# A fused attention and two-layer kernel: the first layer's inner columns in groups of 2, 2, 3, 3, 3 and 3 chunks

## Chip, cores and metric

The kernel runs on one core of a Trainium2 chip. The metric is the device time of one execution in microseconds (us); the number given for a kernel is the median of its runs. The trace is that of one profiled execution.

## What is computed

Linear attention over 4 sequences of 576 tokens and 8 heads of 64 (no softmax), a root-mean-square norm for each head, then a dense layer with an ELU, then four experts of which every token uses all, weighted by given probabilities:

```
kv  = einsum('bhsd,bhse->bhde', k, v);  o = einsum('bhsd,bhde->bhse', q, kv)
x   = o / sqrt(mean(o*o) + 1e-6) * g_norm          # 2304 tokens x 512
h   = x @ w_in                                      # 512 -> 2048
y   = elu(h) @ w_out                                # 2048 -> 512
out = sum_e p[:, e] * (relu(y @ w1[e]) @ w2[e])     # 512 -> 1024 -> 512, 4 experts
```

The weights `w_in` and `w_out` of the first layer arrive as 64-bit floats. All products are made from float32 operands split into a high part and a rest, so that a product takes three matmuls.

## The kernel before

Tokens go in 6 blocks of 384 (`NB` = 6, `T` = 384). The first layer's 2048 inner columns are 16 chunks of 128. `first_groups` says which chunks are summed in PSUM before the sum is added to the accumulator in SBUF: before, [0, 1], [2, 3], [4 to 7], [8 to 11], [12 to 15]. Group 0 runs inside the attention stage, whose order is written out by hand (`plan`). The other groups run in one list of steps: for each group, for each block j, for each chunk c of the group one step, 84 in all. A step is `emit_mm1` (12 matmuls of 384 columns into a bank of "ab", lines 425 to 427; then the ELU: ScalarE at lines 434 and 435, VectorE at line 439 in `end_elu`; then the split of the result into two parts, ScalarE at line 186, GpSimd at line 196) and, two steps later (`LAG`), `emit_mm2` (12 matmuls into four banks, lines 463 to 465). At a group's first chunk of a block `emit_mm2` takes four of the six banks "efghcd" in turn; at its last chunk `into_acc` adds the four banks to the accumulator of the block, one VectorE instruction each (line 457; for group 0 a ScalarE copy, line 455). I call this the turnover of a block.

The weights of a chunk are two pieces (`w_in` and `w_out`, 128 x 512). A piece is loaded into one of two `raw` buffers (line 140, queue of SyncE), turned from 64-bit to 32-bit floats by five VectorE instructions (lines 154, 157, 171, 179, 182) and two of ScalarE (165, 166), and split into a slot of the pool `w_p` (ScalarE line 186, GpSimd line 196). `w_p` has 17 slots (`NSLOT`). They also hold the second layer's weights: `stage_w1` makes sums of blocks of `w1` in one slot (`tf`, lines 219 to 222), `split_w1` fills four, `split_w2` one for each piece of `w2`, and the two sums `s` of `make_forms` take one each. A slot of the first layer comes free when the last block has used its piece.

`todo` holds what is emitted among the steps, by half step h: the pieces of the next group during a group, and during the last group the first preparation of the second layer. That is `stage_w1`/`split_w1` for the first two half groups of expert columns, `split_w2` for two pieces, and `one_form`, five times. `make_forms(0)` makes seven matrices (A11, S2, S1, A12, S3, A22, S4) from the finished accumulators of blocks 0 and 1, splits each on ScalarE (line 186) and GpSimd (line 196) into half of an `x_p` buffer, which it shares with the blocks' inputs `xq`, and stores each to DRAM. The second layer begins with `emit_q(0, 0, 0)`, whose first products (lines 505 to 507) read these forms. The place in `todo` sets a rank, not a time: the order on each engine is fixed when the program is built, and work whose inputs and buffers are there may stand ahead of its place.

Of the kernel before, what the change touches and what calls it, by code (L numbers as in the profile page):

```python
# [33 lines left out]
def attention_moe_kernel(  # L34
# [25 lines left out]
    NF = FG // P  # L60
# [6 lines left out]
    NB = NT // T  # L67
# [57 lines left out]

    w_in, w_out = w_in.bitcast(U32), w_out.bitcast(U32)
    NC1 = F1 // P
    first_groups = [[0, 1], [2, 3]] + [list(range(n, n + NF)) for n in range(NF, NC1, NF)]
    assert sum(map(len, first_groups)) == NC1
    NG = E * F2 // FG  # L130

# [592 lines left out]
    steps = []  # L724
    for g, cs in list(enumerate(first_groups))[1:]:
        begins = 2 * len(steps)
        steps += [(g, j, c) for j in range(NB) for c in cs]
        length = 2 * len(steps) - begins
        if g + 1 < len(first_groups):
            cs = first_groups[g + 1]  # L730
            pieces = [p for i in range(0, len(cs), 2) for p in ((0, cs[i]), (0, cs[i + 1]), (1, cs[i]), (1, cs[i + 1]))]
            for n, (ab, c) in enumerate(pieces):
                todo.setdefault(begins + length * (n + 3) // (len(pieces) + 4), []).append((split_w, 0, ab, c))
    def one_form():
        next(forms_of_0, None)

    for h, ops in ((6, [(stage_w1, 0, 0), (split_w1, 0, 0)]), (22, [(one_form,)]), (24, [(one_form,)]),
                   (28, [(one_form,)]), (32, [(one_form,)]), (36, [(one_form,)]),
                   (40, [(stage_w1, 0, 1), (split_w1, 0, 1)]), (46, [(split_w2, 0, 0)]), (48, [(split_w2, 0, 1)])):
        todo.setdefault(begins + h, []).extend(ops)  # L740

    forms_of_0 = make_forms(0)
# [102 lines left out]
```

## Time and profile before

| | us |
|---|---|
| median of 3 runs | 1224.46 (1224.4 to 1226.63) |
| profiled execution, its own time | 1225.07 |
| its span, first to last instruction | 1223.3 |
| TensorE (PE) busy in the span | 1205.8 |
| VectorE (DVE) busy | 627.8 |
| ScalarE (ACT) busy | 444.0 |
| GpSimd (POOL) busy | 350.4 |

The profiled execution took 1.8 us more than its span and 0.6 us more than the median. PEld in the rows is TensorE's weight load, SP the queue of SyncE. Matmuls are pipelined, so the busy time of one is about twice the distance from one to the next; lost time is better read from the number of matmuls in a stretch.

### The profile page before, as it was taken

What the parts mean: (1) busy time and instruction counts of PE and PEld (TensorE: products, weight loads), DVE (VectorE), ACT (ScalarE), POOL (GpSimd) and SP (SyncE); (2) the same over time, 40 slices, a digit from 0 to 9 for tenths busy, and PEclk for the clock granted to TensorE, in tenths of its full rate; (3) what the DMA queues carried; (4) which work ended last, traced back from release to release, by engine and by line L of the source; (5) the groups of instructions that cost most, each with busy time, mean ns of one, the idle gap of its engine ahead of it and who ended that gap; (6) DMA issues with size and microseconds to landing.
All of it is one profiled execution on the core that took longest, in us unless ns stands there. A gap on an engine that the chain in (4) does not pass through costs nothing.

```text
span 1223.3 us, 16937 instructions
## 1 busy us (share of the span) xinstructions
PE 1205.8 (99%) x6678; PEld 1122.4 (92%) x6678; DVE 627.8 (51%) x1071; ACT 444.0 (36%) x858; POOL 350.4 (29%) x311
## 2 busy tenths in 40 slices
PE   8899999999999999999999999999999999999998
PEld 8799999999999999999999999999999999999997
DVE  5777888474222526755445445445445445444443
ACT  3667666454344544332132132122123123122110
POOL 1223454253233744452032033023023023021000
PEclk9999999999999999999999999999999999999999
DMA  9611333120000312443442442441451451450562
GB/s 332 220 52 53 87 86 103 37 61 10 1 18 27 138 55 80 200 158 101 172 151 84 183 158 72 179 178 54 175 202 36 188 207 35 190 201 15 206 233 77
DMA packets 43887, 147.14 MB, mean 120 GB/s; under 512 B 7072, under 2 KB 7072, under 8 KB 43808
## 3 DMA queue, kind: packets, MB, share of 16 engines
q1 hardware_dynamic: 43808, 146.07, 33.6%
q8 instruction: 52, 0.85, 0.3%
q14 instruction: 27, 0.22, 0.1%
HBM read 124.82 MB, written 21.23 MB: 119 GB/s over the span
## 4 chain that ended last, share of the span: by engine, by line
PE 79%; DVE 2%; ACT 1%; issue 1%; DMA 0%; POOL 0%; DVEq 0%; POOLq 0%; ACTq 0%
PE ps_y L559 11%; PE ps_y L558 11%; PE ps_y L560 11%; PE ps_h L425 3%; PE ps_h L427 3%; PE ps_h L426 3%; PE ps_y L465 3%; PE ps_y L464 3%; PE ps_y L463 3%; PE ps_a L505 3%; PE ps_c L506 3%; PE ps_a L507 3%; PE ps_c L507 3%; PE ps_a L506 3%; PE ps_c L505 3%; PE ps_b L506 3%
## 5 line engine op out<-in xcount | busy, mean ns | idle before, releaser
L559 PE MATMUL ps_y<-w,h 128*128 128x512 f32 x576 | 226.2, 393 | 0.0
L558 PE MATMUL ps_y<-w,h 128*128 128x512 f32 x576 | 224.0, 391 | 0.4 <-DVE acc L571 0.4
L560 PE MATMUL ps_y<-w,h 128*128 128x512 f32 x576 | 220.1, 391 | 0.0
L532 POOL TENSOR_TENSOR c<-u,p 128x384 f32<-128x384 f32 x48 | 49.2, 1026 | 418.7 <-DVE h L544 418.7
L544 DVE SCALAR_TENSOR_TENSOR h<-c,h 128x384 fp32r<-128x384 f32 x144 | 97.6, 677 | 136.5 <-ACT h L543 136.5
L196 POOL TENSOR_TENSOR h<-e,h 128x384 fp32r<-128x384 f32 x96 | 104.0, 1085 | 197.8 <-ACT h L186 171.2
L543 ACT ACTIVATE h<-c 128x384 fp32r<-128x384 f32 x144 | 75.8, 527 | 199.3 <-POOL c L532 77.0
L425 PE MATMUL ps_h<-x,w 128*128 128x384 f32 x384 | 129.8, 338 | 1.4 <-DVE e L439 1.2
L465 PE MATMUL ps_y<-h,w 128*128 128x384 f32 x384 | 129.1, 336 | 0.7 <-POOL w L196 0.7
L463 PE MATMUL ps_y<-h,w 128*128 128x384 f32 x384 | 124.8, 338 | 5.0 <-DVE acc L457 2.5
L426 PE MATMUL ps_h<-x,w 128*128 128x384 f32 x384 | 128.5, 335 | 0.5 <-DVE x L401 0.5
L464 PE MATMUL ps_y<-h,w 128*128 128x384 f32 x384 | 128.8, 335 | 0.0
L427 PE MATMUL ps_h<-x,w 128*128 128x384 f32 x384 | 128.4, 334 | 0.0
L560 PEld LDWEIGHTS ps_y<-w,h 128*128 128x128 f32 x576 | 108.1, 188 | 21.7
L558 PEld LDWEIGHTS ps_y<-w,h 128*128 128x128 f32 x576 | 108.1, 188 | 19.6 <-DVE acc L571 0.8
L559 PEld LDWEIGHTS ps_y<-w,h 128*128 128x128 f32 x576 | 108.0, 188 | 19.4
L571 DVE SCALAR_TENSOR_TENSOR acc<-ps_y,p_sb,acc 128x512 f32<-128x512 f32 x126 | 87.6, 746 | 65.2 <-PE ps_y L560 65.1
L439 DVE SCALAR_TENSOR_TENSOR e<-e,ps_h 128x384 f32<-128x384 f32 x96 | 52.7, 550 | 114.9 <-ACT e L435 114.8
L521 ACT COPY p<-ps_c 128x384 f32<-128x384 f32 x48 | 23.1, 482 | 153.4 <-PE ps_c L507 153.4
L463 PEld LDWEIGHTS ps_y<-h,w 128*128 128x128 f32 x384 | 71.9, 188 | 7.2 <-DVE acc L457 3.8
L434 ACT ACTIVATE e<-ps_h 128x384 f32<-128x384 f32 x96 | 46.8, 487 | 84.9 <-PE ps_h L427 82.0
L425 PEld LDWEIGHTS ps_h<-x,w 128*128 128x128 f32 x384 | 72.1, 188 | 4.0 <-DVE e L439 3.6
(103 smaller groups left out, 2381.8 us busy)
## 6 DMA issues: line engine op xcount, KB each, us to landing
f<-kept SPq DMA_DIRECT2D x98, 768.0 KB, 7.5
raw<-in_moe_w_dram SPq DMA_DIRECT2D x64, 256.0 KB, 2.7
kept<-f SPq DMA_DIRECT2D x21, 768.0 KB, 3.3
raw<-in_moe_w_in_dram SPq DMA_DIRECT2D x16, 512.0 KB, 3.6
raw<-in_moe_w_out_dram SPq DMA_DIRECT2D x16, 512.0 KB, 3.7
qkv<-in_k_dram SPq DMA_DIRECT2D x18, 256.0 KB, 5.8
qkv<-in_v_dram SPq DMA_DIRECT2D x18, 256.0 KB, 5.6
qkv<-in_q_dram SPq DMA_DIRECT2D x18, 256.0 KB, 5.4
```

The lines of the kernel that those rows point to most:

```text
L196: eng.tensor_tensor(out=l, in0=x, in1=h, op=ALU.subtract)
L425: nc.tensor.matmul(ps, ah, bh, start=(kk == 0), stop=False)
L426: nc.tensor.matmul(ps, ah, bl, start=False, stop=False)
L427: nc.tensor.matmul(ps, al, bh, start=False, stop=(kk == KD - 1))
L463: nc.tensor.matmul(ps, bh[:, cols], hi, start=first, stop=False)
L464: nc.tensor.matmul(ps, bh[:, cols], lo, start=False, stop=False)
L465: nc.tensor.matmul(ps, bl[:, cols], hi, start=False, stop=last)
L506: nc.tensor.matmul(ps, wh, xl, start=False, stop=False, skip_group_check=True)
L544: nc.vector.scalar_tensor_tensor(out=lo, in0=ps, scalar=0.0, in1=hi.bitcast(F32), op0=ALU.max, op1=ALU.subtract,)
L558: nc.tensor.matmul(ps, hi[:, cols], bh, start=first, stop=False)
L559: nc.tensor.matmul(ps, hi[:, cols], bl, start=False, stop=False)
L560: nc.tensor.matmul(ps, lo[:, cols], bh, start=False, stop=last)
```

## The change

The inner groups become [4 to 6], [7 to 9], [10 to 12] and [13 to 15], so that there are six groups in place of five. The list that spreads the next group's pieces is written so that a group of odd length fits: the pieces of a pair of chunks, then those of the single one. The preparation of the second layer keeps its start, which is counted from the end of the list of steps as before (24 steps from the end), though the last group now begins 6 steps later; its five calls of `one_form` move from half steps 22, 24, 28, 32 and 36 to 28, 30, 32, 35 and 38, and the second `stage_w1` from 40 to 42.

```diff
-    first_groups = [[0, 1], [2, 3]] + [list(range(n, n + NF)) for n in range(NF, NC1, NF)]
+    first_groups = [[0, 1], [2, 3]] + [list(range(n, n + 3)) for n in range(4, NC1, 3)]
...
-            pieces = [p for i in range(0, len(cs), 2) for p in ((0, cs[i]), (0, cs[i + 1]), (1, cs[i]), (1, cs[i + 1]))]
+            pieces = [(ab, c) for i in range(0, len(cs), 2) for ab in (0, 1) for c in cs[i:i + 2]]
             for n, (ab, c) in enumerate(pieces):
                 todo.setdefault(begins + length * (n + 3) // (len(pieces) + 4), []).append((split_w, 0, ab, c))
+    begins = 2 * (len(steps) - NB * NF)
...
-    for h, ops in ((6, [(stage_w1, 0, 0), (split_w1, 0, 0)]), (22, [(one_form,)]), (24, [(one_form,)]),
-                   (28, [(one_form,)]), (32, [(one_form,)]), (36, [(one_form,)]),
-                   (40, [(stage_w1, 0, 1), (split_w1, 0, 1)]), (46, [(split_w2, 0, 0)]), (48, [(split_w2, 0, 1)])):
+    for h, ops in ((6, [(stage_w1, 0, 0), (split_w1, 0, 0)]), (28, [(one_form,)]), (30, [(one_form,)]),
+                   (32, [(one_form,)]), (35, [(one_form,)]), (38, [(one_form,)]),
+                   (42, [(stage_w1, 0, 1), (split_w1, 0, 1)]), (46, [(split_w2, 0, 0)]), (48, [(split_w2, 0, 1)])):
         todo.setdefault(begins + h, []).extend(ops)
```

## Rows read from the trace of the kernel before

**Rows 1.** The page's first part: busy time, share of the span, instructions.
```profile
PE 1205.8 (99%) x6678; PEld 1122.4 (92%) x6678; DVE 627.8 (51%) x1071; ACT 444.0 (36%) x858; POOL 350.4 (29%) x311
```

**Rows 2.** Busy time (and instructions) of PE, PEld, DVE, ACT, POOL by stretch.
```profile
122.00:174.00 52.00, 49.83 (x282) 48.38 (x281) 44.22 (x77) 31.01 (x59) 24.04 (x20) 1.00 0.32 91
174.00:228.00 54.00, 52.72 (x297) 50.87 (x296) 42.89 (x71) 34.84 (x66) 24.63 (x21) 1.00 0.30 89
228.00:250.00 22.00, 22.00 (x129) 22.00 (x128) 5.25 (x10) 8.32 (x17) 6.45 (x7) 1.00 0.00 1
250.00:280.00 30.00, 29.98 (x173) 29.66 (x172) 24.84 (x38) 19.01 (x37) 16.62 (x13) 1.00 0.25 70
280.00:400.00 120.00, 120.00 (x694) 120.00 (x693) 32.30 (x61) 46.93 (x93) 39.47 (x39) 1.00 0.04 12
400.00:434.00 34.00, 33.64 (x195) 33.26 (x194) 17.49 (x24) 18.04 (x34) 25.39 (x24) 1.00 0.37 145
434.00:472.00 38.00, 37.94 (x219) 37.62 (x219) 12.35 (x24) 15.85 (x32) 17.02 (x16) 1.00 0.15 45
```

**Rows 3.** Waits of PEld from 122 to 472: total us, times, longest.
```profile
PEld ps_y L463 <- DVE acc L457: 3.8, 4, 1.5
PEld ps_h L425 <- DVE e L439: 3.6, 8, 0.8
```

**Rows 4.** VectorE's groups from 122 to 228: busy us, mean ns, idle before.
```profile
L457 DVE TENSOR_TENSOR acc<-ps_y,acc 128x384 f32<-128x384 f32 x36 | 18.7, 547 | 0.0
L179 DVE SCALAR_TENSOR_TENSOR x<-raw,x 128x512 uint32<-128x512 uint32 x19 | 15.5, 815 | 2.7 <-ACT x L166 2.7
L182 DVE SCALAR_TENSOR_TENSOR m<-m,x 128x512 f32<-128x512 f32 x18 | 13.6, 755 | 0.1
L171 DVE SCALAR_TENSOR_TENSOR m<-raw,m 128x512 f32<-128x512 uint32 x17 | 12.8, 754 | 0.1
L439 DVE SCALAR_TENSOR_TENSOR e<-e,ps_h 128x384 f32<-128x384 f32 x23 | 12.6, 546 | 0.3 <-ACT e L435 0.3
L154 DVE TENSOR_SCALAR x<-raw 128x512 uint32<-128x512 uint32 x18 | 11.9, 664 | 0.3
L157 DVE TENSOR_SCALAR m<-raw 128x512 uint32<-128x512 uint32 x16 | 10.4, 652 | 14.5 <-DMA raw<-in_moe_w_out_dram 5.8 <-POOL w L196 5.3 <-DMA raw<-in_moe_w_in_dram 3.4
```

**Rows 5.** Timeline of VectorE, 167 to 173: start, us, instruction, idle before.
```profile
167.20 0.42 DVE L154 TENSOR_SCALAR x<-raw 128x512 uint32<-128x512 uint32 x1
170.19 0.43 DVE L157 TENSOR_SCALAR m<-raw 128x512 uint32<-128x512 uint32 x1 [2.57 <-DMA raw<-in_moe_w_out_dram]
...
171.74 0.55 DVE L457 TENSOR_TENSOR acc<-ps_y,acc 128x384 f32<-128x384 f32 x1
172.21 0.68 DVE L182 SCALAR_TENSOR_TENSOR m<-m,x 128x512 f32<-128x512 f32 x1
```

**Rows 6.** Timeline of PE in the same place.
```profile
170.87 0.34 PE L465 MATMUL ps_y<-h,w 128*128 128x384 f32 x1
172.35 0.44 PE L463 MATMUL ps_y<-h,w 128*128 128x384 f32 x1 [1.14 <-DVE acc L457]
```

**Rows 7.** All adds to the accumulators: duration min/median/max, first and last start.
```profile
L457 DVE TENSOR_TENSOR acc<-ps_y,acc x96: 540/551/559, 124.9 to 471.8; 128x384 f32<-128x384 f32 x96
```

**Rows 8.** Timeline of GpSimd: the split of a first-layer piece on either side of its pause.
```profile
213.23 1.28 POOL L196 TENSOR_TENSOR w<-m,w 128x512 fp32r<-128x512 f32 x1 [2.48 <-PE ps_y L465]
251.13 1.29 POOL L196 TENSOR_TENSOR w<-m,w 128x512 fp32r<-128x512 f32 x1 [1.90 <-ACT w L186]
```

**Rows 9.** First sum of the forms (VectorE) and last split of a form (GpSimd).
```profile
407.24 1.49 DVE L272 TENSOR_TENSOR s<-acc 128x768 f32<-128x768 f32 x1
430.17 1.98 POOL L196 TENSOR_TENSOR f<-s,f 128x384 fp32r<-128x384 f32 x2 [0.80 <-ACT f L186]
```

**Rows 10.** First matmuls of the second layer, timeline of PE.
```profile
465.71 0.33 PE L505 MATMUL ps_a<-f,w1f 128*128 128x384 f32 x1
471.49 0.44 PE L505 MATMUL ps_a<-f,w1f 128*128 128x384 f32 x1
```

## Prediction

> **What bounds the kernel now.** I read the page's first part, then the busy times by stretch of the first layer, then the waits of TensorE in it, and last the timelines where it waits. The first part says that TensorE is the bound: it is busy for 1205.8 of 1223.3 us [rows 1], the others for half of the span or less. The change leaves every matmul as it is, so it can only move the time that TensorE loses, and only where the groups 1 and later run, from about 122 to 472 us.
>
> How much that is, I take from counts of matmuls [rows 2]. From 280 to 400 us there are 694 in 120 us, 0.1729 us each, and TensorE is never idle: that is its full pace here, and a step of 24 matmuls takes 4.15 us. At this pace 52 us hold 300.7 matmuls; from 122 to 174 there are 282, so 18.7 x 0.1729 = 3.2 us are lost. From 174 to 228, 312.3 less 297 gives 2.6 us. From 228 to 250 nothing is lost, from 250 to 280 0.1, from 400 to 434 0.3, from 434 to 472 0.1. The sum is 6.3 us, and 5.8 of it lie before 228. A few records can be missing, which would make it smaller; the waits of the weight loads, 3.8 and 3.6 us [rows 3], give about the same by another way. So no regrouping can win more than some 6 us, 0.5%.
>
> Why it is lost there: until 228 us VectorE turns weight pieces into float32 as fast as the buffers allow. It is busy for 44.2 of 52 us and 42.9 of 54 [rows 2], and the five lines of a piece take 0.82 + 0.76 + 0.75 + 0.66 + 0.65 = 3.6 us, 18 times in 106 us [rows 4], one each 5.9 us. The order on VectorE is fixed, so what TensorE needs stands behind a piece. The largest case shows it: VectorE had nothing from 167.6 to 170.2 but waited for a raw piece's DMA, then worked on that piece, and the first add of a turnover came at 171.74 [rows 5]; TensorE, whose last matmul of the block had begun at 170.87, began the next block at 172.35 [rows 6]. Four turnovers lost 3.8 us, the ELU's end 3.6 us in eight waits [rows 3]. There were 36 adds, nine turnovers, from 122 to 228 [rows 4], so a turnover beside the pieces lost 3.8 / 9 = 0.42 us on the mean, 1.5 us at most.
>
> **The change part by part.**
>
> *Turnovers.* Each of six blocks gets one more: 6 x 4 = 24 adds more, at 0.551 us [rows 7] 13.2 us of VectorE. It is busy for about half of the span and these adds lie beside matmuls, so the 13.2 us themselves are not on the path. They would be, one for one, only where VectorE has no room left. From 174 to 228 it works 42.9 of 54 us; turnovers come every 3 steps (12.45 us) in place of 4 (16.6 us), 4.3 in place of 3.25, so 1.1 x 4 x 0.551 = 2.4 us more, 45.3 of 54. That is the share it has from 122 to 174, so it fits. What it costs TensorE: 1.1 turnovers x 0.42 = +0.5 us. Bounds: 0, when all are hidden, as all are from 280 to 400; 1.1 x 1.5 = 1.7 us if each is as bad as the worst.
>
> *The stretch before 174.* Group 1 is as before: same steps, turnovers and slots. Its six pieces are the first of the former eight, and the seventh follows from the next group, because pieces run ahead of their places: piece 17 of the 24 that belong to groups 2 and later, the first of group 4, was split at 213 us [rows 8], though its place lies inside group 3, which begins only after the pause that these rows show. So the 3.2 us lost there stay, with a different order inside. I take 0, between -1.6 (half of it) and +1.5 (one worst wait more).
>
> *Slots.* Between 213.23 and 251.13 us no piece was split [rows 8]: eight slots of group 2, eight of group 3 and one of group 4 fill the 17. The pause ends when the last block has used the first piece of group 2. With three chunks the last block starts 5 x 3 = 15 steps into the group, not 20, so 5 x 4.15 = 20.8 us earlier: the pieces go on at about 230. Six slots come free, pieces 18 to 23 run from there to about 251, and the last waits for group 3, 18 steps or 75 us later, about 304. The work of 250 to 280 moves to 230 to 255; there it met two turnovers and lost 0.1 us, and meets two again. Cost 0; cover is one piece in a step of TensorE, as the slots set it, and if that were gone the price of two turnovers is 2 x 0.42 = 0.8 us. A gain is excluded where nothing is lost. The DMAs of the pieces are as many, in the same queue, and only move with them.
>
> *The forms and the second layer's start.* The sums of the forms wait for block 1's last turnover. They began at 407.24 and the last form was split at 430.17 + 1.98 = 432.15 [rows 9], 25 us later. Block 1 now ends 12 steps before the end of the list in place of 16, so 4 x 4.15 = 16.6 us later: 424 to 449. Ahead of the sums nothing is lost, since A11 and A12 need block 0 alone (also 16 to 20 us later, about 409). The second layer first reads them at 465.7 and goes over to them wholly at 471.5 [rows 10]. There are 17 us in hand and GpSimd, busy for 25.4 of 34 us in that work and 17.0 of 38 after it [rows 2], has the room; queued behind the forms on GpSimd are the splits of h that `emit_mm2` reads. The work of 400 to 434 lost 0.3 us; moved, it loses the same, and has one turnover more beside it. I take 0, bounds -0.3 and +0.8. Weight slots are no shorter: last group and first half group need 6 + 4, not 8 + 4, of 17, so the second half group's five and the pieces of `w2` come into slots sooner.
>
> Sum: +0.5 us, bounds about -1.9 and +4.8 if all ends fell together; the terms are independent, so -0.7 to +2.1 for this case. The profiled execution would go from 1225.07 to 1225.6, its span from 1223.3 to 1223.8. The median of the runs is 0.6 us below the profiled one, so 1224.46 + 0.5 = **1225.0**, own range 1223.8 to 1226.6.
>
> The Trainium skill, in "Perfetto Trace Analysis" under "Matmuls", would have independent groups of matmuls rotate through PSUM banks so that the evacuation of one lies beside the next group's matmuls. That is how the six banks are used here, and by that rule the added turnovers are free and the sum is 0; the trace has five of nine turnovers that agree and four that waited, up to 1.5 us.
>
> **The rivals.**
>
> *Turnovers all hidden.* For it: from 228 to 400 us no turnover waits. Against: the four that did. A sum of 0, or down to -1.9 with a better order in group 1: 1222.6 to 1224.5.
>
> *The pieces fall into a better order (faster).* The waits come from pieces that stand ahead of an add or an ELU end while their DMA is under way (14.5 us of VectorE's idle time ahead of line 157 [rows 4]). If the shorter list for group 1 moves two or three of these waits off the path, half of the 5.8 us goes: -2.9, so 1221.6. Against: the supply of pieces is set by two raw buffers and the slots, which don't change before 213 us. It decides from 2.4 us on.
>
> *VectorE too full from 174 to 250 (slower).* The pieces now run through with only a short pause at 213 to 230, and turnovers come more often. If the load of 122 to 174, where 3.2 us in 52 were lost, holds from 174 to 252, the loss there is 78 x 3.2 / 52 = 4.8 us in place of 2.6 + 0.1: +2.1, and with one worst wait at a turnover +3.6: 1228.1. It decides when more than 2.4 us come in addition. For it: 45.3 of 54 us of work; against: group 1 has a turnover every 8.3 us.
>
> *Forms late.* If the chain of sums and splits took over 42 us and not 25, TensorE would wait at 471 for each us of it; 5 us late gives 1229.5. Against: the 17 us in hand.
>
> **How the numbers follow.** Likeliest case 45%; turnovers hidden 18%; better order 17%; VectorE too full 15%; forms late 5%. A measurement here tells about 0.2%, 2.4 us, from no change, so 1222.0 to 1226.9 counts as no change: the first two cases, 63%. Faster 17%, slower 20%. The range 1222.3 to 1227.6 leaves out most of the better order below and the worst of the last two above, together about 2 in 10.
>
> **What would show it.** In the trace after: 120 adds of 0.55 us at line 457, in place of 96; PE's count in 122 to 174 near 282 again, and in 174 to 228 within some 6 of 297; splits of pieces between 230 and 251 us and one near 304; the first sum of the forms near 424 and the last split near 449; PE's first wholly second-layer stretch near 472. The prediction is wrong if waits of PE on line 457 or 439 between 122 and 255 grow or shrink by more than 2.4 us, if PE waits for a form or a `w1f` at 472, or if something past 472 moves, where I expect nothing.

## The result, and the profile after

The changed kernel takes 1231.64 us (median of 6 runs, 1230.29 to 1233.76), the kernel before 1224.74 in the same measurement: a ratio of 1.0052, 95% interval 1.0041 to 1.0063. It is slower by 6.9 us at the medians; the forecast was no change, 1225.0, and the range ended at 1227.6. The spans are 1229.8 and 1223.3 us.

Busy time by stretch of the changed kernel (PE, PEld, DVE, ACT, POOL, granted clock, DMA share, GB/s), to hold against [rows 2]:

```profile
122.00:174.00 52.00, 50.44 (x287) 49.19 (x286) 44.62 (x78) 31.47 (x60) 25.06 (x21) 1.00 0.31 92
174.00:228.00 54.00, 52.41 (x292) 49.99 (x291) 45.07 (x74) 34.49 (x64) 24.25 (x20) 1.00 0.30 88
228.00:280.00 52.00, 50.72 (x292) 50.27 (x292) 31.73 (x52) 26.30 (x51) 22.98 (x19) 1.00 0.13 41
280.00:400.00 120.00, 120.00 (x695) 120.00 (x693) 36.50 (x73) 46.57 (x92) 34.55 (x34) 1.00 0.02 5
400.00:434.00 34.00, 34.00 (x198) 34.00 (x198) 15.08 (x22) 17.57 (x33) 17.16 (x17) 1.00 0.21 84
434.00:472.00 38.00, 34.67 (x183) 34.22 (x182) 13.75 (x26) 15.50 (x31) 24.24 (x24) 0.91 0.33 113
```

One stretch stands out: 183 matmuls from 434 to 472 us where [rows 2] have 219, and a granted clock of 0.91. TensorE at its full pace does 0.1729 us a matmul, so those 36 are 6.2 us, nearly the whole difference of the spans (6.5). Up to 280 us it lost little more than before: counted in one window from 122 to 280, 868 matmuls and not 875, 1.2 us. From 280 to 434 it even has four more.

Timelines of TensorE and of GpSimd in that stretch, changed kernel:

```profile
437.00 0.51 PE L463 MATMUL ps_y<-h,w 128*128 128x384 f32 x2
440.84 0.69 PE L464 MATMUL ps_y<-h,w 128*128 128x384 f32 x1 [3.33 <-POOL h L196]
441.33 0.52 PE L465 MATMUL ps_y<-h,w 128*128 128x384 f32 x1
441.65 0.52 PE L464 MATMUL ps_y<-h,w 128*128 128x384 f32 x1
```
```profile
427.37 2.37 POOL L196 TENSOR_TENSOR f<-s,f 128x384 fp32r<-128x384 f32 x2 [1.81 <-ACT f L186]
429.70 2.36 POOL L196 TENSOR_TENSOR f<-acc,f 128x384 fp32r<-128x384 f32 x2
432.01 2.02 POOL L196 TENSOR_TENSOR w1f<-raw,w1f 128x512 fp32r<-128x512 f32 x1
434.00 1.98 POOL L196 TENSOR_TENSOR f<-s,f 128x384 fp32r<-128x384 f32 x2
435.93 3.23 POOL L196 TENSOR_TENSOR w1f<-tf,w1f 128x512 fp32r<-128x512 f32 x2
439.12 0.72 POOL L196 TENSOR_TENSOR w1f<-raw,w1f 128x256 fp32r<-128x256 f32 x1
439.81 0.98 POOL L196 TENSOR_TENSOR h<-e,h 128x384 fp32r<-128x384 f32 x1
```

GpSimd works for 12.4 us without a pause on six splits of forms and four of `w1f` before it comes to the split of h that `emit_mm2` waits for. TensorE stands for 3.33 us, and then its matmuls follow each other by 0.32 us (441.33, 441.65). The view of busy times over just that piece shows the reason, a granted clock of 0.51, the lower of the two levels (1.2 GHz):

```profile
441.00:447.20 6.20, 6.20 (x20) 6.20 (x21) 3.06 (x6) 3.39 (x7) 6.20 (x7) 0.51 0.59 217
447.20:452.00 4.80, 4.80 (x30) 4.80 (x29) 0.56 (x1) 1.64 (x3) 2.86 (x4) 1.00 0.64 208
```

Twenty matmuls took 6.2 us, 2.7 more than at the full pace. The wait and the slow clock after it make 6.0 us. The kernel before lost a little here too: of the 428 matmuls that 400 to 474 us could hold it has 423, the changed kernel 391, so the net loss is 32 matmuls, 5.5 of the 6.5 us.

The same place in the kernel before, GpSimd: four splits of forms and two of `w1f`, then h, after 7.9 us.

```profile
409.73 2.36 POOL L196 TENSOR_TENSOR f<-s,f 128x384 fp32r<-128x384 f32 x2 [1.81 <-ACT f L186]
412.05 1.47 POOL L196 TENSOR_TENSOR w1f<-raw,w1f 128x512 fp32r<-128x512 f32 x1
413.48 2.89 POOL L196 TENSOR_TENSOR f<-s,f 128x384 fp32r<-128x384 f32 x2
416.33 1.29 POOL L196 TENSOR_TENSOR w1f<-tf,w1f 128x512 fp32r<-128x512 f32 x1
417.58 1.01 POOL L196 TENSOR_TENSOR h<-e,h 128x384 fp32r<-128x384 f32 x1
```

### The profile page after: what moved, and what is told of

It is laid out like the page before. It is cut to its first block, busy times and chain, and to the rows that moved or that the text cites. A ratio compares the mean times of both kernels' runs of the same rounds, so it can differ in the third digit from the quotient of the medians.

```text
span 1229.8 us, 16956 instructions
## 1 busy us (share of the span) xinstructions
PE 1208.3 (98%) x6678; PEld 1124.4 (91%) x6678; DVE 638.3 (52%) x1095; ACT 444.4 (36%) x858; POOL 349.1 (28%) x311
## 4 chain that ended last, share of the span: by engine, by line
PE 85%; DVE 7%; DMA 4%; POOL 1%; ACT 1%; issue 1%; SPq 0%; DVEq 0%; ACTq 0%; POOLq 0%
PE ps_y L559 11%; PE ps_y L558 11%; PE ps_y L560 11%; PE ps_y L465 4%; PE ps_y L464 4%; PE ps_y L463 4%; PE ps_h L426 4%; PE ps_h L425 4%; PE ps_h L427 4%; PE ps_a L505 3%; PE ps_a L507 3%; PE ps_a L506 3%; PE ps_c L506 3%; PE ps_c L507 3%; PE ps_c L505 3%; PE ps_b L506 3%
## 5 line engine op out<-in xcount | busy, mean ns | idle before, releaser
L457 DVE TENSOR_TENSOR acc<-ps_y,acc 128x384 f32<-128x384 f32 x120 | 62.8, 551 | 48.3 <-PE ps_y L465 48.2
```

## The experiments

The stage up to 110 us, whose order all but the raw buffers' edits leave alone, took a different time from one profiled execution to another: its granted clock was 0.94 to 1.00, and the first add of line 457 (458 where the edit adds a line) began between 123.6 and 128.3 us. So I compare TensorE's matmuls in the stretches 122 to 280 us (full: 914) and 400 to 474 us (full: 428), and give the ratio to the kernel before for the whole. The kernel before, then the changed one:

```profile
122.00:280.00 158.00, 154.53 (x875) 150.91 (x874) 117.20 (x195) 93.18 (x177) 71.74 (x59) 1.00 0.26 74
400.00:474.00 74.00, 73.58 (x423) 72.87 (x422) 31.54 (x50) 34.49 (x68) 42.40 (x39) 1.00 0.26 92
```
```profile
122.00:280.00 158.00, 153.57 (x868) 149.44 (x867) 121.43 (x202) 92.25 (x174) 72.29 (x59) 1.00 0.25 74
400.00:474.00 74.00, 70.67 (x391) 70.22 (x391) 29.12 (x48) 34.10 (x65) 43.33 (x40) 0.95 0.28 97
```

The first count varies too: the changed kernel and the five experiments that leave its order up to 280 us alone have 860 to 868.

**Are the new places of the forms the cause?** No run was made: the kernel before with the new half steps is built to the same order on every engine as with the old, and the changed kernel with its forms spread over 28 to 42 to the same as with 28 to 38. The old places can't be tried in the changed kernel: block 1's last add is emitted at half step 27, and the sums that read it would stand at 22. Behind that add the places are inert; what moved the work is what it waits for.

**The pile on GpSimd: the four splits moved to VectorE.** In `split_w1`, for g = 0 and f = 1:

```diff
+        eng = nc.vector if (g, f) == (0, 1) else nc.gpsimd
...
-            split(hi, lo, src, nc.gpsimd)
+            split(hi, lo, src, eng)
```

> The changed kernel, with the second half group's w1f splits (four instructions) on VectorE, not GpSimd. Theory A (the loss is a pile on GpSimd near 430 to 440: six splits of forms and four of w1f stand ahead of a split of h, TensorE waits 3.3 us for it and then runs 20 matmuls at half clock): six instructions are left ahead of it, the wait falls under 0.5 us, the clock stays at 1.00, and the time falls by about 6 us to 1225.6 (1224.5 to 1226.5). Rival B (the three-chunk groups cost it through VectorE: 24 adds more, more turnovers): VectorE gets 5 us more work there, so the time stays at 1230 to 1232 or rises.

Measured: 1.0052 (1.0037 to 1.0067), as the changed kernel, and 406 matmuls in the second stretch. The waits of TensorE from 400 to 474 us (the edit adds a line, so L440 is the end of the ELU):

```profile
PE ps_h L426 <- DVE e L440: 3.5, 2, 2.6
```

My number failed. The wait on h is gone, but the splits now stand ahead of the ELU's end on VectorE, and TensorE waits there for nearly as long; rival B's time came, by these splits and not by the turnovers that it named. The clock stayed at 1.00, so 15 of the 37 lost matmuls came back in this stretch, 2.6 us. The whole does not show them. In the profiled execution a longer first stage hides them (the first add of line 458 began at 128.1 us, that of line 457 in the changed kernel at 124.3). But of the four runs even the one with the highest mean clock, 0.999, took 1230.67 us; why stays open.

**The order alone.** The work stays on GpSimd; the four splits are put behind the last split of h that is emitted before their place (first edit), or each behind one of four consecutive earlier ones (second edit, k = 0 to 3, steps 75 to 78):

```diff
+        last_h = on_pool()[-1]
...
+            tc.add_manual_dep(i, last_h.name, ...)           # first edit
...
+            tc.add_manual_dep(i, h_split[75 + k].name, ...)  # second edit
```

> The changed kernel with the same work on GpSimd, but the second half group's four w1f splits ordered behind the splits of h that are emitted before their place. Theory A: only the order counts, so the wait near 440 falls under 0.5 us, and the time falls to about 1225.6 (1224.5 to 1227). Rival C (GpSimd has too much work in that stretch whatever the order): the wait moves to a later split of h, and the time stays above 1229.

Measured: 1.0106 (1.0091 to 1.0121). Busy time by stretch, then the waits of TensorE from 476 to 520 us:

```profile
400.00:474.00 74.00, 74.00 (x428) 73.87 (x428) 30.07 (x49) 34.47 (x65) 41.04 (x39) 1.00 0.24 87
491.00:498.00 7.00, 4.95 (x15) 4.16 (x16) 4.34 (x10) 2.84 (x5) 0.95 (x1) 0.76 0.55 225
```
```profile
PE ps_y L560 <- DVE h L544: 2.6, 1, 2.6
PE ps_y L558 <- ACT h L543: 1.5, 1, 1.5
```

The old wait is wholly gone, 428 of 428, with six splits of forms still in a row there. But now the four splits come late, from 463.09 to 467.58 us, and hold the raw buffers that they read: the queue of SyncE waited 17.2 us for one of them ahead of a load. The loads that follow are late, and in the second layer a sum on VectorE waits for one, ahead of the part of h that TensorE needs:

```profile
489.39 0.43 DVE L219 TENSOR_TENSOR tf<-raw 128x256 f32<-128x256 f32 x1 [3.46 <-DMA raw<-in_moe_w_dram]
...
491.27 0.55 DVE L544 SCALAR_TENSOR_TENSOR h<-c,h 128x384 fp32r<-128x384 f32 x1
```

TensorE waits at 491 and again falls to a lower clock. This chain is read from the rows; no run tested it.

> The changed kernel, same work on GpSimd, with the four w1f splits of the second half group ordered each behind a later split of h (one of four consecutive ones), so neither ahead of all of them nor behind all. Theory A (the order on GpSimd is the whole loss after 400 us): TensorE loses under 1 us from 434 to 472, the clock stays at 1.00, no wait for w1f near 490, and the time is 1.0005 to 1.002 of the kernel before, some 5 to 6 us under the changed kernel. Rival C (too much work in the stretch whatever the order): the wait shows up at another split, and the ratio stays above 1.004.

Measured: 1.0015 (1.0003 to 1.0027), 424 matmuls in the second stretch and no wait from there to 520 us but one of 0.4. GpSimd, with one foreign split or two between the splits of h:

```profile
437.67 1.01 POOL L196 TENSOR_TENSOR h<-e,h 128x384 fp32r<-128x384 f32 x1
438.64 1.29 POOL L196 TENSOR_TENSOR w1f<-raw,w1f 128x512 fp32r<-128x512 f32 x1
439.89 1.03 POOL L196 TENSOR_TENSOR h<-e,h 128x384 fp32r<-128x384 f32 x1
440.86 1.30 POOL L196 TENSOR_TENSOR w1f<-tf,w1f 128x512 fp32r<-128x512 f32 x1
```

So the order on GpSimd is the loss after 400 us, and a remainder of 0.15% lies elsewhere.

**Why the splits stood there: the slots.** First with 15 slots throughout (`NSLOT = 15`), then with two or four of the 17 held by idle tiles, from just ahead of the sums until block 2 is done:

```diff
+            held.append(w_p.tile([P, 2, 512], F32, tag="w", name="held"))   # 2 or 4 of them
+            nc.vector.memset(held[-1][:, 0, :1], 0.0)
...
+            nc.vector.tensor_tensor(out=t[:, 0, :1], in0=acc[2][:, 0, :1], in1=acc[2][:, 1, :1], op=ALU.add)
```

> The changed kernel with 15 weight slots in place of 17. Theory A: with two slots fewer the third and fourth w1f split wait again for the slots of the sums, as in the kernel before, so eight instructions and not ten stand ahead of the split of h, 2.3 us less work; the wait falls from 3.3 to about 1 us, too short for a drop of the clock, and the time falls to about 1226.5 (1225.5 to 1228). Rival B: fewer slots help nothing, first-layer pieces pause earlier, 1231 to 1233.

Measured: 1.0035 (1.0024 to 1.0047). That lies between the two forecasts. The waits on h are shorter but two, the clock stays at 1.00, and 412 matmuls fit in the second stretch:

```profile
PE ps_y L464 <- POOL h L196: 2.2, 2, 1.4
```

> The changed kernel, with two weight slots held by idle tiles from just ahead of the forms' sums until block 2's accumulator is done, so that as many slots are free there as in the kernel before; nothing else moves. Theory A with slots as the reason (free slots let the third and fourth w1f split in ahead of the splits of h): eight instructions are left ahead of the late split of h and not ten, its wait falls from 3.3 to 1 to 1.7 us, the clock stays at 1.00, TensorE loses 2 to 3 us from 400 to 474 in place of 5.5, as with 15 slots, and the ratio to the kernel before falls from 1.005 to about 1.003. If the 15 slots helped by something else (the earlier pause of the pieces), the wait stays at 3.3 us with the drop of the clock, and the ratio at 1.005.

Measured: 1.0037 (1.0025 to 1.0048), the same two waits, 2.2 us, 409 matmuls.

> The same with four slots held, so that no w1f split gets in before block 2 is done. Slots as the reason: the wait near 440 is gone (six splits of forms alone ahead of it), the four w1f splits come together after 444 and may cost a split of h there 1 to 2 us; 1.0015 to 1.003 of the kernel before. Otherwise: 1.005.

Measured: 1.0010 (1.0000 to 1.0019). TensorE waits for nothing:

```profile
400.00:474.00 74.00, 74.00 (x429) 73.88 (x428) 33.53 (x59) 36.18 (x71) 46.44 (x43) 1.00 0.29 101
```

None, two and four slots taken away give 3.3, 2.2 and 0 us of waiting. The fewer slots were free, the better the kernel ran: it was the free ones that let the `w1f` splits in ahead of h.

**The pieces before 280 us: a third raw buffer.** The raw pool gets three buffers, the weight slots go to 16 (with four buffers: 15):

```diff
-    NSLOT = 17
+    NSLOT = 16
...
-    raw_p = ctx.enter_context(tc.tile_pool(name="raw", bufs=2))
+    raw_p = ctx.enter_context(tc.tile_pool(name="raw", bufs=3))
```

With the splits on VectorE:

> As the first of these, with a third raw buffer and 16 weight slots in place of 17. If VectorE's waits for a raw piece's DMA make the 5 to 7 us that TensorE loses from 122 to 255 us, those waits ahead of line 157 (some 10 us) shrink to below 3 and the time falls 2 to 3 us under the first of these, to about 1223. If VectorE's own load makes the loss, the pieces only bunch, and the time is that of the first within 1 us.

Measured: 1.0012 (1.0002 to 1.0021); 879 matmuls from 122 to 280 us and 412 after 400, where the first experiment had 867 and 406. With the splits one by one:

> The one before with three raw buffers and 16 weight slots. If the raw buffers hold up the pieces from 122 to 255 us: 2 to 3 us less, 0.998 to 1.000 of the kernel before. If VectorE's own work does: the ratio of the one before within 0.0008.

Measured: 0.9987 (0.9978 to 0.9996).

> The splits one by one, with four raw buffers and 15 weight slots. If more raw buffers go on helping: another 1 us under that with three. If 15 slots stop the pieces too early (the pause comes two pieces sooner): 0.5 to 2 us over it.

Measured: 0.9988 (0.9979 to 0.9998): neither, a fourth buffer and 15 slots leave it as it was. With the groups of the kernel before:

> The kernel before (groups of four) with three raw buffers and 16 weight slots. If the third raw buffer is what helps, whatever the groups: 0.997 to 0.999 of the kernel before. If groups of four need the seventeenth slot: pieces and w1f splits wait for slots, and the ratio is 1.000 or above.

Measured: 0.9970 (0.9959 to 0.9980), 1222.72 against 1226.43 us, the fastest of the study and faster than both kernels. Busy time from 122 to 280 us, groups of three with three raw buffers (splits one by one), then groups of four with three:

```profile
122.00:280.00 158.00, 154.58 (x878) 151.43 (x877) 124.62 (x205) 93.17 (x177) 70.97 (x59) 1.00 0.24 72
```
```profile
122.00:280.00 158.00, 157.38 (x899) 155.19 (x898) 118.01 (x196) 94.55 (x180) 72.00 (x60) 1.00 0.24 71
```

Before, with two buffers, it was 875. So the third buffer is worth 24 matmuls, 4.1 us, with groups of four, and with it the groups of three cost 21, 3.6 us, in this stretch; after 400 us they have six more here, and the medians, 1224.84 and 1222.72, differ by 2.1 us. The edit also takes a slot, but slots alone did little: 15 slots with two raw buffers gave 872 matmuls in this stretch, 4 more than the changed kernel. What VectorE waits for ahead of a piece (line 157) in this stretch, first in the changed kernel, then in the groups of four with three buffers:

```profile
  DMA raw<-in_moe_w_out_dram: 7.9, 5
  DMA raw<-in_moe_w_in_dram: 5.1, 3
  POOL w L196: 3.4, 4
```
```profile
  POOL w L196: 12.3, 11
```

In the kernel before, the three are 7.6, 3.4 and 5.6 us. The waits for the DMA are gone; VectorE now waits for the split of an earlier piece (two buffers `m`), and TensorE loses less beside it.

## Why the prediction was wrong, point by point

*What bounds the kernel.* Right: TensorE's pace is the same, and the whole difference is time that it lost between 122 and 474 us. Wrong in one sentence of it: I read from the loss of the kernel before how much could be won, and let it stand for how much was at stake. Nothing limited the loss.

*The forms and the second layer's start* is the step that failed: "I take 0, bounds -0.3 and +0.8". It measured 32 matmuls by the count over 400 to 474 us, 5.5 us. The times in it were right (first sum of the forms at 424.89, foreseen 424), and it named the splits of h that are queued behind the forms. But it priced GpSimd by its share of busy time, 25.4 of 34 us, where a queue in fixed order is priced by the longest run of foreign work ahead of the one instruction that TensorE needs: 12.4 us in place of 7.9. And it counted earlier slots as harmless ("come into slots sooner"). In the kernel before, the third `w1f` split had to wait for a slot, that of a sum whose last reader is the split of a form on GpSimd, and the fourth stands behind it. ScalarE's part of that third split, kernel before:

```profile
423.23 0.63 ACT L186 CAST w1f<-tf 128x512 fp32r<-128x512 f32 x1 [2.34 <-POOL f L196]
```

This wait kept the two out of GpSimd's way. Shown by the held slots and by the order alone. That the pair for A22 (the two halves of one form) also came earlier is seen in the rows; why is not shown. By itself it cost nothing: in the experiments that keep the `w1f` splits back, TensorE lost nothing with six splits of forms in a row.

The drop of the clock was in no term and no bound. It is 2.7 of the 6.0 us. The waits of 1.4 us at most, in the experiments with 15 slots or two held, came without it, and so did one of 2.57 us with the splits on VectorE.

The Trainium skill, in "SBUF — State Buffer" under "Who interferes with whom", says that a VectorE instruction with two SBUF inputs contends with a GpSimd instruction that reads SBUF. The trace agrees: the `w1f` split that lies beside a sum of line 272 took 2.02 us, the same one beside nothing of that kind, in the order one by one, 1.29. The two at 435.93, beside another such sum, took 3.23, where two elsewhere take 2.59. Two pairs of forms beside the sums of lines 219 to 222 took 2.37 and 2.36, a pair elsewhere 1.98. Together that is 2.1 of the 12.4 us, an estimate from these rows; by the same reckoning it is 1.5 of the 7.9 us in the kernel before, so it makes little of the difference.

*Turnovers and slots* were mis-sized. I took +0.5 for the added turnovers and 0 for the moved pieces; 122 to 280 us lost 1.2 us more, up to 2.6 in the experiments with the same order there (860 to 868 matmuls after 875), and with the order mended the whole remainder is 0.15%, 1.8 us. I priced a turnover by the waits at line 463. They did not grow: 2.1 us of PE's waits in five, after 2.5 in four. What grew was the wait for the end of the ELU, 2.4 us in three waits after 0.9 in two. VectorE and TensorE of the changed kernel at the largest:

```profile
249.88 1.01 DVE L457 TENSOR_TENSOR acc<-ps_y,acc 128x384 f32<-128x384 f32 x2
250.81 0.68 DVE L171 SCALAR_TENSOR_TENSOR m<-raw,m 128x512 f32<-128x512 uint32 x1
251.41 0.68 DVE L179 SCALAR_TENSOR_TENSOR x<-raw,x 128x512 uint32<-128x512 uint32 x1
252.02 0.54 DVE L457 TENSOR_TENSOR acc<-ps_y,acc 128x384 f32<-128x384 f32 x1
252.48 0.54 DVE L439 SCALAR_TENSOR_TENSOR e<-e,ps_h 128x384 f32<-128x384 f32 x1
```
```profile
253.07 0.44 PE L425 MATMUL ps_h<-x,w 128*128 128x384 f32 x1 [1.28 <-DVE e L439]
```

Three adds and two instructions of a piece stand ahead of the end of the ELU. The adds delay what is queued behind them, not only the banks that they free. The place is the one where the pieces, resumed 21 us sooner (split at 230.03, foreseen 230), meet the turnovers; there I had put 0.

*What held:* the stretch before 174 us (287 matmuls, expected near 282), the 24 adds at 0.55 us, the pieces' pause and their end at 306.52 (foreseen 304), and no new wait of TensorE after the second layer had begun. VectorE was busy for 45.1 of 54 us from 174 to 228, foreseen 45.3. The rival "VectorE too full", the nearest to the measured time that had its loss there, foresaw +2.1 us; TensorE has five matmuls fewer, 0.9 us. None of the named signs of a wrong prediction came, neither the waits on lines 457 and 439 (they grew by 1.1 us) nor one for a form at 472: the loss lay where no sign looked. The rival "better order" had no place in the change; its mechanism, pieces that wait for a raw buffer ahead of what TensorE needs, was real, and the third buffer paid 4.1 us by it. Of the rival "forms late" the place was wrong: TensorE waited at 441 for h, not at 472 for a form.

What stays open: how much of the 21 matmuls between groups of three and four is the adds themselves and how much the order that they force on VectorE; no run parted them.

## What to carry to other kernels

Where the order on an engine is fixed, find for each edit the longest run of foreign work ahead of the instruction that the bound engine waits for; the busy share does not show it. A buffer that comes free sooner is not free of cost: a full pool may be what spaces the work out, so ask what will rush in. And a wait on TensorE may cost nearly twice, once as itself and once in the clock after it: here the one of 3.33 us did, and those of 1.4 us did not.

## What the runs showed of the hardware that was not expected

After 3.33 us without a matmul the granted clock stood at 0.51 for 6.2 us and then went back to 1.00; two waits of at most 1.4 us within 3 us of each other left it at 1.00, and so did one of 2.57 us in the first experiment. In the experiment with the splits behind the last h, waits of 2.56 and 1.18 us with one matmul between them were followed by matmuls 0.32 us apart, at a mean clock of 0.76 from 491 to 498. And the stage up to 110 us, in one order in the changed kernel and in the first experiment, had 906 matmuls at a clock of 0.98 in the profiled execution of one and 886 at 0.94 in that of the other:

```profile
0.00:110.00 110.00, 100.40 (x906) 94.15 (x907) 77.89 (x158) 64.28 (x123) 21.50 (x27) 0.98 0.50 173
```
```profile
0.00:110.00 110.00, 100.77 (x886) 93.77 (x887) 76.10 (x153) 61.40 (x117) 21.00 (x26) 0.94 0.49 173
```

The first layer's first add by VectorE comes 3.8 us later in the second, about the size of the effects looked for, and the reason for comparing stretches. The kernel before alone, in one measurement of 28 runs, went from 1223.33 us at a mean clock of 1.000 to 1228.18 at 0.994.
